# The second layer's matmuls in two halves of 112 columns

## The chip, the core and the metric

The kernel runs on one core of one Trainium2 chip. The metric is the device time of one execution in microseconds (us), median of three runs. The matmuls are float32 throughout.

## The reference

Eight batches of attention with RMS-normed queries and keys, followed by a two-layer block on the 3584 resulting rows of 768 values:

```python
# q, k, v: (8, 12, 448, 64)
q_n, k_n = rmsnorm(q, g_q), rmsnorm(k, g_k)
scores = q_n @ k_n.T / sqrt(64)
attn = softmax(scores)
x = (attn @ v) -> (8 * 448, 12 * 64)

# w_in: (768, 2048), w_out: (2048, 768)
h = x @ w_in
g = h - tanh(h)
out = g @ w_out
```

The first layer is `x @ w_in`, the second `g @ w_out`.

## The kernel before

From the second batch on, both layers are computed with a Strassen-like scheme: the tokens of a batch (448) and the two other dimensions are split in halves, and seven products of half the size in each direction take the place of eight. Each product is a run of matmuls with 128x128 weights and `HS` = 224 columns of tokens, which accumulate in one bank of PSUM. The weights' combinations lie in DRAM and come through a ring of six buffers. In the first batch the second layer is computed without the scheme (`project_first`, line 675, 448 columns).

The matmuls of both layers are issued by one generator, `products`. `layer` is 0 for the first layer (4 blocks `j`, `width` 2, `depth` 3) and 1 for the second (3 blocks `j`, `width` 1, `depth` 8). `moving[p]` gives the tokens' side of product `p`: for the second layer slices of `g` (tile gT) and their combinations (tile tg).

```python
HS = S // 2                                  # 224
ORDER = (1, 5, 6, 2, 3, 7, 4)

def products(b, layer, count, width, depth, moving, done_with):
    took = 4 * HS / ENGINE_NS
    ...
    def product(j, p, bank, first):
        if b == 0:
            ...
        else:
            ring_load(ring_steps.index((b, layer, j, p)) + 5)
            w = ring_tiles[b, layer, j, p].rearrange("p (n d) -> p n d", d=P)
        for f in range(width):
            for c in range(depth):
                nc.tensor.matmul(                                   # line 510
                    bank[:, f * HS : (f + 1) * HS], lhsT=w[:, c * width + f, :], rhs=moving[p](c),
                    start=(first and f == 0 and c == 0), stop=(f == width - 1 and c == depth - 1),
                    skip_group_check=not first,
                )
                if f < width - 1 or c < depth - 1:
                    yield took
    ...
    for j in range(count):
        use = done_with(j)
        for p in ORDER:
            first = p not in (2, 3, 7)
            bank = banks[p] = mm_bank() if first else banks[{2: 1, 3: 5, 7: 6}[p]]
            yield from product(j, p, bank, first)
            use(p, bank)
            yield took
```

The generator is advanced piece by piece between the parts of the attention of the batch ahead, by an estimate of time, not by what is ready:

```python
def run(ns):
    spent[1] += ns
    while spent[0] + 1.0 < spent[1]:
        took = next(stream, None)
        if took is None:
            return
        spent[0] += took

def slot(s):                       # one step of attention, two heads
    gap = gap_ns(s)
    totals(s, sc_bank())           # line 443: sums of the softmax
    if has(s + 1):
        scores(s + 1, 0)           # line 401: 112x448, 64 rows
    ...
    run(gap)
    if has(s + 2):
        turn(s + 2, sc_bank(), sc_bank())      # lines 377 and 381: transposes, 112 columns
    ...
    run(gap)
    divide(s, values(s, sc_bank()))            # line 429: attn @ v
    ...
    run(gap)
    ...
    run(gap)
```

The transposes are matmuls of TensorE too: the block to be turned is the weights' operand, and an identity of 112 columns is the moving one.

Of the kernel before, what the change touches and what calls it, by code (L numbers as in the profile page):

```python
# [92 lines left out]
def bounded_path(tc, ctx, q, k, v, moe_w_in, moe_w_out, out, g_col, ident, ones, neg_half):  # L93
# [16 lines left out]
    nc = tc.nc  # L110
# [12 lines left out]
    HS = S // 2  # L123
# [25 lines left out]
    def mm_bank():  # L149
        return ps_m.tile([P, 512], F32, name="mm")  # L150
# [34 lines left out]
    def built(j, p):  # L185

        if j == 2:
            return ring[:, p * 2 * HALF : (p + 1) * 2 * HALF].rearrange("p (f n) -> p f n", f=2)
        return w_half[j == 1][p]
# [51 lines left out]
    def weight(to):  # L241

        while done[1] < min(to, PIECES):
            n = done[1]
            round_weight_a(nc, raws[n], weight_dst(n))
            if n:
                round_weight_b(nc, raws[n - 1], weight_dst(n - 1))
            done[1] = n + 1
            finish_weights(n)
            while done[0] < min(n + 4, PIECES) and place_free(done[0]):  # L250
                weight_load(done[0])
                done[0] += 1
            if kept[1] < kept[0] and n >= 4 * kept[0] + 2:
                keep_weights()
        if done[1] == PIECES > done[2]:
            round_weight_b(nc, raws[PIECES - 1], weight_dst(PIECES - 1))
            finish_weights(PIECES)
# [15 lines left out]
    def combine(count):  # L273
        for j, p, dst, x, y, op in combos[:count]:
            nc.vector.tensor_tensor(out=dst, in0=x, in1=y, op=op)  # L275
            if p == 7:
                kept[0] = j + 1
        del combos[:count]
# [51 lines left out]
    def ring_load(to):  # L330

        for n in range(len(ring_tiles), min(to, len(ring_steps))):
            b, layer, j, p = ring_steps[n]
            t = ring_tiles[ring_steps[n]] = ring_slot()
            if layer == 0:
                assert kept[1] > j
                nc.sync.dma_start(out=t[:, : 2 * HALF], in_=w_in_dram[j, p])
            else:
                nc.sync.dma_start(out=t, in_=w_out_dram[:, BLOCKS[p], j].rearrange("p f d -> p (f d)"))
# [149 lines left out]
    def products(b, layer, count, width, depth, moving, done_with):  # L489

        took = 4 * HS / ENGINE_NS
        banks = {}

        def product(j, p, bank, first):
            if b == 0:
                weight(due[7 * j + ORDER.index(p)])  # L500
                combine(1)
                while any(c[:2] == (j, p) for c in combos):
                    combine(1)
                w = built(j, p).rearrange("p f (n d) -> p (f n) d", d=P)
            else:
                ring_load(ring_steps.index((b, layer, j, p)) + 5)
                w = ring_tiles[b, layer, j, p].rearrange("p (n d) -> p n d", d=P)
            for f in range(width):
                for c in range(depth):
                    nc.tensor.matmul(  # L510
                        bank[:, f * HS : (f + 1) * HS], lhsT=w[:, c * width + f, :], rhs=moving[p](c),
                        start=(first and f == 0 and c == 0), stop=(f == width - 1 and c == depth - 1),
                        skip_group_check=not first,
                    )
                    if f < width - 1 or c < depth - 1:
                        yield took
            now = late["todo"]
            late["todo"] = []
            for fn in now:
                fn()  # L520
# [9 lines that stand above are left out]
# [570 lines left out]
```

## Time and profile before

| | before |
|---|---|
| time, median of 3 runs | 1482.98 us (1481.69 to 1483.19) |
| span of the profiled execution | 1479.9 us |
| TensorE: matmul busy | 1442.1 us, 97% |
| TensorE: weight load busy | 1142.9 us, 77% |
| VectorE busy | 791.8 us, 54% |
| ScalarE busy | 469.6 us, 32% |
| GpSimd busy | 469.0 us, 32% |
| DMA | 247.32 MB, 167 GB/s |

In the profile PE is TensorE's matmuls and PEld its weight loads, which can lie beside matmuls; DVE is VectorE, ACT ScalarE, POOL GpSimd. A group's row gives line, engine, operation, written tile <- read tiles, the array's rows * columns, the moving operand's partitions x elements, the count, the busy time in us (overlaps counted once), the mean duration of one in ns, and the idle time of the engine just before, with what ended it. A matmul's duration is longer than the time from one to the next, since matmuls are pipelined.

### The profile page before, as it was taken

What the parts mean: (1) busy time and instruction counts of PE and PEld (TensorE: products, weight loads), DVE (VectorE), ACT (ScalarE), POOL (GpSimd) and SP (SyncE); (2) the same over time, 40 slices, a digit from 0 to 9 for tenths busy, and PEclk for the clock granted to TensorE, in tenths of its full rate; (3) what the DMA queues carried; (4) which work ended last, traced back from release to release, by engine and by line L of the source; (5) the groups of instructions that cost most, each with busy time, mean ns of one, the idle gap of its engine ahead of it and who ended that gap; (6) DMA issues with size and microseconds to landing.
All of it is one profiled execution on the core that took longest, in us unless ns stands there. A gap on an engine that the chain in (4) does not pass through costs nothing.

```text
span 1479.9 us, 22097 instructions
## 1 busy us (share of the span) xinstructions
PE 1442.1 (97%) x8520; PEld 1142.9 (77%) x8520; DVE 791.8 (54%) x1165; ACT 469.6 (32%) x850; POOL 469.0 (32%) x336
## 2 busy tenths in 40 slices
PE   6889999999999999999999999999999999999997
PEld 2358744587888788878888887888788878889997
DVE  4889998656543664346534564454555356423322
ACT  6765554233222322232322233223332233200100
POOL 4556664134311343124412243212441134202310
PEclk9999999999999999999999999999999999999999
DMA  9759788854456454645465536545545654465663
GB/s 183 157 154 244 247 238 219 231 169 145 146 171 182 130 175 135 189 136 163 147 177 143 164 127 192 145 127 171 173 147 139 178 167 134 126 177 160 184 195 98
DMA packets 244997, 247.32 MB, mean 167 GB/s; under 512 B 143380, under 2 KB 187156, under 8 KB 244884
## 3 DMA queue, kind: packets, MB, share of 16 engines
q1 hardware_dynamic: 244560, 245.82, 58.0%
q8 instruction: 70, 1.15, 0.3%
q14 instruction: 43, 0.35, 0.1%
q10 hardware_dynamic: 324, 0.00, 0.0%
HBM read 212.34 MB, written 33.42 MB: 166 GB/s over the span
## 4 chain that ended last, share of the span: by engine, by line
PE 86%; DVE 10%; DMA 2%; issue 1%; SPq 0%; POOL 0%; ACT 0%; ACTq 0%; DVEq 0%; POOLq 0%
PE mm L510 60%; PE sc L401 9%; PE sc L429 9%; PE mm L675 3%; DVE sum L420 2%; PE sc L443 2%; DMA q_nat<-in_q_dram 1%; PE sc L381 1%; DVE w_out L79 1%; DVE sum L418 1%; PE sc L377 1%; DVE w_out L82 1%; DVE w_out L78 1%; DVE w_out L275 1%; DVE rr L357 1%
## 5 line engine op out<-in xcount | busy, mean ns | idle before, releaser
L406 ACT ACTIVATE p<-sc,rr 112x448 f32<-112x448 f32 x384 | 212.3, 638 | 480.2 <-PE sc L401 468.2
L510 PE MATMUL mm<-xT,w_f 128*128 128x224 f32 x1392 | 278.8, 355 | 0.0
L510 PEld LDWEIGHTS mm<-xT,w_f 128*128 128x128 f32 x1392 | 260.3, 190 | 17.3 <-issue 12.6
L510 PEld LDWEIGHTS mm<-gT,w_f 128*128 128x128 f32 x1344 | 251.3, 190 | 23.7 <-issue 23.7
L510 PE MATMUL mm<-gT,w_f 128*128 128x224 f32 x1344 | 267.8, 355 | 0.0
L360 POOL TENSOR_TENSOR rr<-rr,neg_half 112x16 f32<-112x16 f32 (+1 forms) x54 | 144.5, 2681 | 259.4 <-DVE rr L359 252.8
L510 PE MATMUL mm<-tt,w_f 128*128 128x224 f32 x1044 | 211.2, 354 | 0.0
L510 PEld LDWEIGHTS mm<-tt,w_f 128*128 128x128 f32 x1044 | 196.1, 190 | 8.0 <-issue 8.0
L510 PE MATMUL mm<-tg,w_f 128*128 128x224 f32 x1008 | 200.4, 353 | 0.0
L510 PEld LDWEIGHTS mm<-tg,w_f 128*128 128x128 f32 x1008 | 189.5, 190 | 0.0
L547 POOL TENSOR_TENSOR gT<-s,th 128x448 f32<-128x448 f32 x96 | 117.3, 1229 | 193.1 <-ACT th L546 192.4
L401 PE MATMUL sc<-qT,kT 64*112 64x448 f32 x768 | 176.3, 573 | 1.6 <-ACT p L406 1.0
L456 DVE TENSOR_TENSOR xT<-sc,rs 64x224 f32<-64x224 f32 x168 | 65.2, 388 | 140.7 <-PE sc L429 137.0
L470 POOL TENSOR_TENSOR tt<-xT,tt 128x224 f32<-128x224 f32 x23 | 15.8, 688 | 391.1 <-DVE xT L456 391.0
L401 PEld LDWEIGHTS sc<-qT,kT 64*112 64x112 f32 x768 | 63.8, 177 | 95.1 <-issue 82.4
L429 PE MATMUL sc<-p,v_nat 112*32 112x448 f32 x1344 | 135.0, 542 | 0.0
L420 DVE TENSOR_TENSOR sum<-sum,p 112x896 f32<-112x896 f32 x78 | 103.0, 1320 | 6.5 <-DVE sum L420 0.5
L429 PEld LDWEIGHTS sc<-p,v_nat 112*32 112x32 f32 x1344 | 39.4, 109 | 74.8 <-issue 73.2
L546 ACT ACTIVATE th<-s 128x448 f32<-128x448 f32 x96 | 55.3, 579 | 106.0 <-DVE s L576 47.6
L675 PE MATMUL mm<-gT,w_out 128*128 128x448 f32 x192 | 74.6, 543 | 0.4 <-POOL w_out L90 0.4
L629 DVE TENSOR_TENSOR s<-mm,s 128x224 f32<-128x224 f32 x21 | 8.2, 392 | 116.2 <-PE mm L510 116.2
L448 DVE RECIPROCAL rs<-sc 128x224 f32<-128x224 f32 x42 | 65.2, 1553 | 1.5 <-PE sc L443 1.2
(97 smaller groups left out, 1323.1 us busy)
## 6 DMA issues: line engine op xcount, KB each, us to landing
w_f<-w_in SPq DMA_DIRECT2D x196, 384.0 KB, 3.7
w_f<-w_out SPq DMA_DIRECT2D x147, 512.0 KB, 4.6
w_raw<-in_moe_w_out_dram SPq DMA_DIRECT2D x16, 768.0 KB, 5.3
k_nat<-in_k_dram SPq DMA_DIRECT2D x96, 112.0 KB, 3.4
q_nat<-in_q_dram SPq DMA_DIRECT2D x48, 224.0 KB, 4.3
v_nat<-in_v_dram SPq DMA_DIRECT2D x48, 224.0 KB, 4.8
out_dram<-th SPq DMA_DIRECT2D x192, 56.0 KB, 2.3
w_in<-w_out SPq DMA_DIRECT2D x21, 384.0 KB, 7.0
```

The source lines that it names most:

```text
L360: nc.gpsimd.tensor_tensor(out=r, in0=r, in1=neg_half[:, : r.shape[1]], op=ALU.pow)
L401: nc.tensor.matmul(sc[:CP, :S], lhsT=kT[r, c * CP : (c + 1) * CP], rhs=qT[r, :], start=True, stop=True)
L406: nc.scalar.activation(p[:, h, i, :], tiles[h][:CP, :S], AF.Exp, scale=rr[:, 0, 2 * c + h : 2 * c + h + 1])
L420: nc.vector.tensor_tensor(out=t, in0=t, in1=part, op=ALU.add)
L429: nc.tensor.matmul(av[r : r + BL, :S], lhsT=v_nat[:, h, c, m * BL : (m + 1) * BL], rhs=p[:, h, c % 2, :], start=(c == 0), stop=(c == NCH - 1),
L443: nc.tensor.matmul(dn[r : r + BL, :HS], lhsT=ones[:CP, :BL], rhs=p[:, h, n * HS : (n + 1) * HS], start=(i == 0), stop=(i == len(parts) - 1),)
L448: nc.vector.reciprocal(rs, dn[:, :HS])
L456: nc.vector.tensor_tensor(out=x[m * D : (m + 1) * D, n * HS : (n + 1) * HS], in0=av[m * D : (m + 1) * D, n * HS : (n + 1) * HS], in1=rs[n ...
L510: nc.tensor.matmul(bank[:, f * HS : (f + 1) * HS], lhsT=w[:, c * width + f, :], rhs=moving[p](c), start=(first and f == 0 and c == 0), sto ...
L546: nc.scalar.activation(th, h, AF.Tanh, bias=0.0, scale=1.0)
L547: eng.tensor_tensor(out=g[:, rows, cols], in0=h, in1=th, op=ALU.subtract)
L675: nc.tensor.matmul(bank[:, :S], lhsT=w_out_row(f, n // HC)[:, n % HC * P : (n % HC + 1) * P], rhs=g[:, f, :], start=(f == 0), stop=(f == C ...
```

## The change

In the second layer of the seven batches that use the seven products, each matmul of 224 columns of tokens becomes two of 112 with the same weights, one for each half of the columns. The two write neighbouring halves of the same stretch of the bank. The first layer, the first batch, the attention and the order of everything else stay as they are. Shorter matmuls give a finer grain: a half's result is there earlier, and the stationary weights serve two matmuls in succession.

```diff
             for f in range(width):
                 for c in range(depth):
-                    nc.tensor.matmul(
-                        bank[:, f * HS : (f + 1) * HS], lhsT=w[:, c * width + f, :], rhs=moving[p](c),
-                        start=(first and f == 0 and c == 0), stop=(f == width - 1 and c == depth - 1),
-                        skip_group_check=not first,
-                    )
+                    m = moving[p](c)
+                    for n in range(0, HS, HS // 2) if layer else (0,):
+                        z = n + HS // 2 if layer else HS
+                        nc.tensor.matmul(
+                            bank[:, f * HS + n : f * HS + z], lhsT=w[:, c * width + f, :], rhs=m[:, n:z],
+                            start=(first and f == 0 and c == 0 and n == 0),
+                            stop=(f == width - 1 and c == depth - 1 and z == HS), skip_group_check=not first,
+                        )
                     if f < width - 1 or c < depth - 1:
                         yield took
```

## The prediction

> **What bounds the kernel now.** I read the page's engine table and slices first, then the chain that ended last, then the list of waits, and then single stretches of the timeline, because the change touches nothing but TensorE and the question is what TensorE's pace consists of.
>
> ```profile
> PE 1442.1 (97%) x8520; PEld 1142.9 (77%) x8520; DVE 791.8 (54%) x1165; ACT 469.6 (32%) x850; POOL 469.0 (32%) x336
> ...
> PEclk9999999999999999999999999999999999999999
> ...
> PE 86%; DVE 10%; DMA 2%; issue 1%; SPq 0%; POOL 0%; ACT 0%; ACTq 0%; DVEq 0%; POOLq 0%
> PE mm L510 60%; PE sc L401 9%; PE sc L429 9%; PE mm L675 3%; DVE sum L420 2%; PE sc L443 2%; DMA q_nat<-in_q_dram 1%; PE sc L381 1%; DVE w_out L79 1%; DVE sum L418 1%; PE sc L377 1%; DVE w_out L82 1%; DVE w_out L78 1%; DVE w_out L275 1%; DVE rr L357 1%
> ```
>
> TensorE is busy 97% of the span at full granted clock, and line 510, the line that is changed, is 60% of the chain. As many weight loads (PEld) as matmuls stand in the table, so every matmul has a load of its own. The list of waits, TensorE alone and from 200 us on, comes to 2.5 us in all:
>
> ```profile
> PE sc L443 <- DVE sum L420: 2.1, 2, 1.6
> PE mm L675 <- POOL w_out L90: 0.4, 1, 0.4
> ```
>
> So after the first batch TensorE runs without a pause. What it gets slower by goes into the time undiminished, and no other engine has to be looked at. The second layer's matmuls are the gT and tg groups:
>
> ```profile
> L510 PE MATMUL mm<-gT,w_f 128*128 128x224 f32 x1344 | 267.8, 355 | 0.0
> L510 PEld LDWEIGHTS mm<-gT,w_f 128*128 128x128 f32 x1344 | 251.3, 190 | 23.7 <-issue 23.7
> L510 PE MATMUL mm<-tg,w_f 128*128 128x224 f32 x1008 | 200.4, 353 | 0.0
> L510 PEld LDWEIGHTS mm<-tg,w_f 128*128 128x128 f32 x1008 | 189.5, 190 | 0.0
> ```
>
> The program has 7 batches x 3 blocks x 7 products x 8 = 1176 such matmul calls, the trace 1344 + 1008 = 2352 records. Each call is thus two passes, and each pass is a load and a matmul. Busy time and duration overlap, so the pace comes from the end of the chain, where line 510 runs alone:
>
> ```profile
> 1334.28 137.93 PE mm L510 x728
> ```
>
> With the last matmul's 0.35 us taken off, 137.58 / 727 = 189.2 ns from one pass to the next. The first batch's matmuls of 448 columns (line 675) follow each other in 376 ns in the trace's records. So a column costs (376 - 189.2) / 224 = 0.834 ns and a pass 2.4 ns besides: the pace is the moving columns', and the load is hidden completely.
>
> **What the Trainium skill says.** "TensorE: Matmul & The Clock Gate", section "LDWEIGHTS (loading the stationary operand)", gives P/1.2 ns for a load of P columns, 107 ns for 128, and the same page, section "Step-by-step: what each phase is for", says that the next tile's weights load while this tile's matmul runs. The trace agrees with both: the load stands beside a 189 ns matmul at no cost, and where it is exposed it costs about what the formula says. In the view of line 510, a matmul's record is 352 ns long in the median and 457 at most:
>
> ```profile
> L510 PE MATMUL mm<-gT,w_f x1344: 352/352/457, 380.2 to 1468.8; 128*128 128x224 f32 x192
> ```
>
> The longest are nearly all the first after the attention's scores (line 401, matmuls on 64 rows), where load and matmul start together in the timeline; the 105 ns more are the load, which nothing hides there. The load's own record of 190 ns is therefore not what it occupies. "Advanced Engine Details and Errata", section "TensorE Details", says that a matmul can start before its load completes. If that held here, those 105 ns would not show; the trace speaks against it for a full 128x128 load.
>
> **The change part by part.** It removes 2352 passes of 224 columns and adds 4704 of 112. The columns streamed are the same; each half brings its weight load again, because a call is a pair of passes with two loads in turn, and the program holds no call without them (the built program has 2352 loads more, as many as matmuls). The order on every engine stays, since the generator yields once per pair and its estimate of the time taken is untouched. DMA, DVE, ACT and GpSimd work is unchanged.
>
> A pass of 112 columns streams in 112 x 0.834 = 93.4 ns, 95.8 with its fixed part. The load for the next pass can begin when the present one starts and needs about 107 ns. For the first time the load is the longer of the two, and the pace becomes the load's. The kernel before contains exactly this pair: the transposes (line 381) are passes of 112 columns, and some are followed at once by a line-510 pass with its 128-column load. Loads at such a place, as the timeline gives them:
>
> ```profile
> 710.29 0.49 PEld L510 LDWEIGHTS mm<-xT,w_f 128*128 128x128 f32 x3
> ```
>
> Three loads of 190 ns cover 0.49 us, so from the first start to the third are 0.30 us. The second of these steps is the ordinary 0.19 us beside a 224-column pass; the first, beside a 112-column transpose, is 0.11. By single records: the transpose starts at 710.289, the load at 710.290, the next load at 710.400, and the matmul between them takes 368 ns instead of 352, 16 ns of waiting for its weights. All 37 such places in the trace give 111 or 112 ns from the transpose to the point where that matmul really streams. I take 111 ns for a pass of the changed stream.
>
> The sum: a pair of halves takes 2 x 111 = 222 ns in place of 189.2, so +32.8 ns, times 2352 = **+77.1 us**. At the ends of the 51 stretches of second-layer work the last half is followed by attention work whose load is short or which has to wait for the matmul's end anyway, so there one half costs 93 to 96 instead of 111: 51 x about 15 ns = -0.8 us. Waits that the slower TensorE could swallow are the 2.5 us above, of which little lies next to the second layer; I count nothing. So +76 us, and 1483 + 76 = 1559; as the loads by themselves are 110 ns apart, which would give +72, I say 1558.
>
> **The rivals.**
> - The load stays hidden, because the second half finds its weights in the array or because a matmul starts on a part of them. A half would then take the 95.8 ns, and the change would cost 2352 x (191.6 - 189.2) = +6 us: 1489, within 2%. For it speaks the skill's sentence and that no call in the kernel before repeats its predecessor's weights at the same place, so that a skipped load could not have been seen. Against it: a call is two passes with two loads, so the weights left in the array at the second half are not those of its first pass; and the 16 ns of waiting at every one of the 37 places.
> - The load is not pipelined at all and holds the array for its 190 ns record. A pair would be 380 ns, +449 us, 1932. Against it stand the overlapping loads just shown, 0.11 us apart.
> - TensorE's instruction supply becomes the bound: two instructions each 111 ns, 55 ns apiece, against 95 before. In attention alone, ahead of the second layer, this stretch did more:
>
> ```profile
> 35.80:47.60 11.80, 11.80 (x128) 5.58 (x130) 10.95 (x20) 10.61 (x20) 5.56 (x4) 1.00 0.64 137
> ```
>
> The first two counts are matmuls and loads: 258 instructions in 11.8 us, 46 ns apiece. The rate is there, though only over 12 us; over a stretch of 150 us it isn't shown. A bound at 60 ns would make it +120 us. The program's own instructions are also fetched by DMA, and 4704 more are some 20% of the 22097; the queue for that takes 0.3% of the transfer time, so I expect nothing.
> - The change helps something: shorter matmuls could release banks sooner or start an eviction earlier. With 2.5 us of waits there is nothing to win; at the very end the last eviction comes after the last half either way.
>
> **Range and chances.** The one uncertain size is the pass of 112 columns. 108.5 ns, the load's bare 107 with a pass's 2 ns, gives +65 us; 112.5 gives +84. With some room for supply, 1549 to 1568 should hold it 8 times in 10. Faster would need a gain that no row offers: 0.01. Within 2%, below 1512.6, is the hidden load: 0.04. Slower by over 2%: 0.95.
>
> **What would show it.** Right: the gT and tg groups with 2688 and 2016 records of 128x112, a pace of 110 to 112 ns for each where they run alone, loads of 190 ns that now overlap each other so that PEld is busy nearly throughout those stretches, matmul records of about 275 ns (the transposes' 259 and 16 of waiting), TensorE still at 97 to 98% and the other engines' busy times unchanged. Wrong: a pace of 96 ns, fewer loads than matmuls, gaps with "issue" ahead of matmuls or loads in those groups, or a granted clock below 1.00.

## The result, and the profile after

The changed kernel takes 1562.4 us (median of 4, 1561.78 to 1564.0) against 1482.8 us of the kernel before (median of 4): 79.6 us more, a ratio of 1.054 (95% interval 1.0522 to 1.0558). The prediction was 1558, with a range of 1549 to 1568.

From the page of the changed kernel, the engine table, the granted clock and the chain that ended last:

```profile
PE 1523.1 (98%) x10872; PEld 1231.0 (79%) x10872; DVE 788.7 (51%) x1165; ACT 469.2 (30%) x850; POOL 469.0 (30%) x336
...
PEclk9999999999999999999999999999999999999999
...
PE 88%; DVE 8%; DMA 1%; issue 1%; ACT 1%; POOL 0%; SPq 0%; ACTq 0%; DVEq 0%; POOLq 0%
```

The only engine whose work grew is TensorE: 81.0 us of matmul busy time and 88.1 us of load busy time. There are 2352 more records of each kind, one load for each added matmul. The line is 513 now. Its second-layer groups (PEld are the loads; count, busy us, mean ns, idle before):

```profile
L513 PEld LDWEIGHTS mm<-gT,w_f 128*128 128x128 f32 x2688 | 304.8, 192 | 23.7 <-issue 16.4
L513 PE MATMUL mm<-gT,w_f 128*128 128x112 f32 x2688 | 313.1, 276 | 0.0
L513 PE MATMUL mm<-tg,w_f 128*128 128x112 f32 x2016 | 234.6, 275 | 0.0
L513 PEld LDWEIGHTS mm<-tg,w_f 128*128 128x128 f32 x2016 | 229.8, 192 | 0.0
```

gT rose from 267.8 to 313.1 us and tg from 200.4 to 234.6: 79.5 us together, as much as the medians differ by. (The two profiled executions differ by 81.3 us; 0.9 us of that is there before the first pass of the second layer's groups.) The idle time ahead of the loads is 23.7 us as before, and no other group grew by more than 0.4 us on the page. The waits of TensorE from 200 us on (us in total, times, longest) come to 2.9 us in place of 2.5:

```profile
PE sc L443 <- DVE sum L420: 2.5, 4, 1.6
PE mm L678 <- POOL w_out L90: 0.4, 1, 0.4
```

So nothing new is waited for; it is the passes that come more slowly. How fast they are can be read in two places. In a stretch of the timeline inside the second layer, loads alone (start and duration in us):

```profile
800.05 0.41 PEld L513 LDWEIGHTS mm<-tg,w_f 128*128 128x128 f32 x3
```

Three loads of 192 ns cover 0.41 us, so they start (0.41 - 0.19) / 2 = 0.11 us apart and each overlaps the next. And at the end of the chain, where line 513 has TensorE to itself:

```profile
1401.33 151.30 PE mm L513 x1120
```

These are 336 passes of 224 columns (the last batch's first layer) and 784 of 112 (its second layer, 672, and the last 112 of the batch ahead). Before, the same work stood there as 728 passes in 137.93 us. The difference is 13.37 us for 392 divided passes: 34.1 ns for each, or (189.2 + 34.1) / 2 = 111.7 ns for a pass of 112 columns. In the records 4614 of 4651 steps inside the two groups are 111 or 112 ns; 36 of the others are 200 ns and follow a first pass whose own load is exposed.

### The profile page after: what moved, and what is told of

Read it like the earlier page. It is cut to its first block, busy times and chain, and to the rows that moved or that the text cites. A ratio compares the mean times of both kernels' runs of the same rounds, so it can differ in the third digit from the quotient of the medians.

```text
span 1561.2 us, 26823 instructions
## 1 busy us (share of the span) xinstructions
PE 1523.1 (98%) x10872; PEld 1231.0 (79%) x10872; DVE 788.7 (51%) x1165; ACT 469.2 (30%) x850; POOL 469.0 (30%) x336
## 3 DMA queue, kind: packets, MB, share of 16 engines
q8 instruction: 88, 1.44, 0.4%
## 4 chain that ended last, share of the span: by engine, by line
PE 88%; DVE 8%; DMA 1%; issue 1%; ACT 1%; POOL 0%; SPq 0%; ACTq 0%; DVEq 0%; POOLq 0%
PE mm L513 63%; PE sc L401 9%; PE sc L429 8%; PE mm L678 3%; PE sc L443 2%; DVE sum L420 2%; PE sc L381 1%; DVE w_out L79 1%; DMA q_nat<-in_q_dram 1%; PE sc L377 1%; DVE w_out L82 1%; DVE sum L418 1%; DVE w_out L78 1%; PE mm L429 1%; DVE rr L357 0%
## 5 line engine op out<-in xcount | busy, mean ns | idle before, releaser
L513 PEld LDWEIGHTS mm<-gT,w_f 128*128 128x128 f32 x2688 | 304.8, 192 | 23.7 <-issue 16.4
L513 PE MATMUL mm<-gT,w_f 128*128 128x112 f32 x2688 | 313.1, 276 | 0.0
L513 PE MATMUL mm<-tg,w_f 128*128 128x112 f32 x2016 | 234.6, 275 | 0.0
L513 PEld LDWEIGHTS mm<-tg,w_f 128*128 128x128 f32 x2016 | 229.8, 192 | 0.0
```

What stands on the lines that cost most here:

```text
L513: nc.tensor.matmul(bank[:, f * HS + n : f * HS + z], lhsT=w[:, c * width + f, :], rhs=m[:, n:z], start=(first and f == 0 and c == 0 and n ...
```

## The experiments

Three readings of these 111.7 ns were put against each other. **L**: a 128-column weight load sets the pace as soon as the moving columns are too few to cover it. **I**: TensorE's instructions can't be supplied faster than about 56 ns each, and there are two to a pass. **F**: a short pass carries a fixed 16 ns whatever its shape. A fourth, **S**, says that it matters that the same weights are loaded twice in a row.

### The pace of passes by shape

The kernel before, with a table of shapes behind its end (results unused):

```diff
     run(1e9)
+    for cols in (128, 96, 64, 32):
+        for n in (224, 160, 128, 112, 64, 32):
+            bank = mm_bank()
+            for i in range(16):
+                nc.tensor.matmul(
+                    bank[:cols, :n], lhsT=ident[:, :cols], rhs=late["g"][:, i, :n], start=(i == 0), stop=(i == 15)
+                )
```

> The kernel before, with 24 groups of 16 matmul calls (32 passes each) put behind its end: weights of 128, 96, 64 and 32 columns, moving operands of 224, 160, 128, 112, 64 and 32. Theory L (the weight load sets the pace of a short pass): a pass takes the longer of the moving columns' time, 0.834 ns each and 2.4 ns, and the load's, 0.834 ns for each weight column and some 5 ns. For 128 weight columns 189, 136, then 112 for 128, 112, 64 and 32 moving columns alike; for 96: 189, 136, 109, 96, then 85 for 64 and 32; for 64: 96 at 112 columns, 58 at 64 and 32; for 32: 96, 56, 31. About 88 us in all, so 1570 us. Rival I (TensorE's supply of instructions, 56 ns for each): no pass under 112 ns at any width of the weights, 99 us in all. Rival F (a fixed 16 ns for a short pass): 112 columns take 112 ns at every width of the weights, 32 columns some 45.

It took 1568.2 us (one run; 1570 were expected). Some groups of the added line; 128*96 means 96 weight columns, the moving operand follows, and busy time less one duration, divided by 31, is the pace (coarse here, because busy time has one decimal):

```profile
L786 PE MATMUL mm<-gT,ident 128*128 128x160 f32 x32 | 4.5, 299 | 0.0
L786 PE MATMUL mm<-gT,ident 128*128 128x112 f32 x32 | 3.7, 275 | 0.0
L786 PE MATMUL mm<-gT,ident 128*128 128x64 f32 x32 | 3.7, 274 | 0.0
L786 PE MATMUL mm<-gT,ident 128*96 128x112 f32 x32 | 3.2, 259 | 0.0
L786 PE MATMUL mm<-gT,ident 128*96 128x64 f32 x32 | 2.9, 247 | 0.0
L786 PE MATMUL mm<-gT,ident 128*64 128x64 f32 x32 | 2.0, 222 | 0.0
L786 PE MATMUL mm<-gT,ident 128*32 128x32 f32 x32 | 1.2, 196 | 0.0
```

With full weights, 64 and 112 moving columns take the same 3.7 us. With 96 weight columns the 112-column group drops to 3.2 us and its matmuls to 259 ns. By single records the median pace in ns is:

| weight columns | 224 moving | 160 | 128 | 112 | 64 | 32 |
|---|---|---|---|---|---|---|
| 128 | 189 | 136 | 112 | 112 | 112 | 112 |
| 96 | 189 | 136 | 109 | 96 | 85 | 85 |
| 64 | 189 | 136 | 109 | 96 | 58 | 58 |
| 32 | 189 | 136 | 109 | 96 | 56 | 32 |

Every entry is that of L within 1 ns. The moving columns cost 0.834 ns each and 2.4 ns; the load costs 0.834 ns a column and 5 ns, which is 111.8, 85.1, 58.4 and 31.7 ns for the four widths; the larger one is the pace. I is out, over stretches as short as these: 32 ns for a pass is 16 ns for an instruction. F is out: 112 columns with 96 weight columns carry no 16 ns.

### Uneven parts

```diff
-                    for n in range(0, HS, HS // 2) if layer else (0,):
-                        z = n + HS // 2 if layer else HS
+                    for n, z in ((0, 160), (160, HS)) if layer else ((0, HS),):
```

> The changed kernel with the halves made uneven, 160 and 64 columns: as many passes, loads and columns. Theory L: the long part takes its columns' 136 ns and hides its load, the short one takes the load's 111.7 ns: 247.5 for both instead of 223.4, times 2352 is +57 us, 1619 us. Rival I: the same, since it is a floor too. Rival F: each part pays for its columns and 16 ns, so the sum is that of the even halves: 1562 us.

Measured: 1617.7 us, ratio to the kernel before 1.0912 (1.0894 to 1.0930). With as many passes, loads and columns as the even halves it is 55.3 us slower than they are. The end of its chain holds the same 1120 passes as that of the changed kernel:

```profile
1445.69 160.74 PE mm L512 x1120
```

160.74 - 151.30 = 9.44 us over 392 pairs is 24.1 ns, exactly 247.5 - 223.4. The long part pays for its columns, the short one for its load, and what the long part has to spare is of no use to the short one. F, which had 1562 us here, is out once more.

### The same weights not twice in a row

Against the changed kernel (the first layer keeps its loop, in an `else` not shown):

```diff
-            for f in range(width):
-                for c in range(depth):
-                    m = moving[p](c)
-                    for n in range(0, HS, HS // 2) if layer else (0,):
-                        ...
+            if layer:
+                for n in (0, HS // 2):
+                    for c in range(depth):
+                        nc.tensor.matmul(
+                            bank[:, n : n + HS // 2], lhsT=w[:, c, :], rhs=moving[p](c)[:, n : n + HS // 2],
+                            ...
+                        )
```

> The changed kernel with the two halves outside the loop over the contraction: first all eight matmuls of one half of the columns, then all eight of the other, so that no two matmuls in a row have the same weights. Theory L: a load costs the same whatever stood in the array before: 1562 us, within 2 us. Rival S (weights that are there already are loaded more cheaply, so the change would have cost more without that; or a repeated load of one place is what costs): more than 5 us away from 1562, in the first case slower, up to the time of a load for every second pass, in the second towards 1489.

Measured: 1562.6 us, ratio 1.0539 (1.0522 to 1.0557), the changed kernel's time to 0.2 us. The two layers have lines of their own here, so the end of the chain separates the first layer (224 columns) and the second (112):

```profile
1413.18 63.58 PE mm L521 x336
1476.76 75.04 PE mm L511 x672
```

63.58 / 336 = 189.2 ns and 75.04 / 672 = 111.7 ns. S is out: with weights that change at every call a pass takes what it takes with weights that come twice.

### The weights in halves instead of the tokens

```diff
-                    nc.tensor.matmul(
-                        bank[:, f * HS : (f + 1) * HS], lhsT=w[:, c * width + f, :], rhs=moving[p](c),
-                        ...
-                    )
+                    for k in range(0, P, P // 2) if layer else (0,):
+                        e = k + P // 2 if layer else P
+                        nc.tensor.matmul(
+                            bank[k:e, f * HS : (f + 1) * HS], lhsT=w[:, c * width + f, k:e], rhs=moving[p](c),
+                            ...
+                        )
```

> The kernel before with the second layer's calls split along the other side: two matmuls of 64 weight columns each, both with all 224 columns of tokens, writing the two halves of the partitions. As many calls, passes and loads as in the changed kernel. Theory L: the loads are half as long and hidden; the two column halves of the array work side by side, as the attention's values do in the trace with four matmuls of 32 weight columns that start 7 ns apart, so a pair takes little more than 189 ns: 1483 to 1500 us. (If the halves did not work side by side it would be about 1930.) Rival I: 4704 passes at 112 ns as in the changed kernel, 1562 us.

Measured: 1487.2 us, ratio 1.0033 (1.0019 to 1.0047). Its groups:

```profile
L512 PE MATMUL mm<-gT,w_f 128*64 128x224 f32 x2688 | 266.3, 354 | 0.0
L512 PE MATMUL mm<-tg,w_f 128*64 128x224 f32 x2016 | 201.4, 353 | 0.0
L512 PEld LDWEIGHTS mm<-gT,w_f 128*64 128x64 f32 x2688 | 190.1, 137 | 81.5 <-issue 16.7 <-PE sc L401 7.3
```

As many passes, loads and instructions as in the changed kernel, but busy times of the kernel before (267.8 and 200.4). The records start in pairs mostly 6 to 8 ns apart, two passes side by side. Four instructions in 189 ns are 47 ns apiece, under the 56 of rival I, and over whole batches: the supply is not what sets the changed kernel's pace. Of the 3.9 us more, 3.0 lie where these stretches meet the transposes: from the last pass to the first transpose 283 ns instead of 189, from the last transpose to the first pass 189 instead of 96, at 16 places each.

This run also shows the load by itself. The longest record, a first pass whose load nothing hides, was 457 ns before, 105 above the median of 352; with half the weight columns it is 52 above:

```profile
L512 PE MATMUL mm<-gT,w_f x2688: 352/352/404, 381.0 to 1472.9; 128*64 128x224 f32 x192
```

So the 105 ns go with the number of weight columns, as a load's time does.

### Dividing where the columns are enough

The second layer of the first batch has matmuls of 448 columns. There the same division can be made with and without dropping below the load:

```diff
-            nc.tensor.matmul(
-                bank[:, :S], lhsT=w_out_row(f, n // HC)[:, n % HC * P : (n % HC + 1) * P], rhs=g[:, f, :],
-                start=(f == 0), stop=(f == CF - 1),
-            )
+            for a in range(0, S, 224):          # 112 in the second run
+                nc.tensor.matmul(
+                    bank[:, a : a + 224], lhsT=w_out_row(f, n // HC)[:, n % HC * P : (n % HC + 1) * P],
+                    rhs=g[:, f, a : a + 224], start=(f == 0 and a == 0), stop=(f == CF - 1 and a + 224 == S),
+                )
```

> The kernel before, with the first batch's second layer (96 calls of 448 columns, 192 passes) in halves of 224 columns; the other batches as before. Theory L: 224 columns hide the load, so a pass of 376 ns becomes two of 189.2 and the cost is 2.4 ns x 192, +0.5 us: the same within 2 us. Rival: halving a matmul costs as such, because the second load has to be paid: 16 ns to 112 ns for each of 192 passes, +3 to +21 us.

> The same calls in four parts of 112 columns. Theory L: 4 x 111.7 in place of 376 ns, +70.8 ns for each of 192 passes: +13.6 us, about 1497 us. A rival in which only the number of passes counts would make this three times the cost of the halves: +1.5 us if those cost 0.5.

In halves of 224: 1482.6 us against 1482.0, ratio 1.0002 (0.9994 to 1.0011). In quarters of 112: 1492.7 us, ratio 1.0073 (1.0059 to 1.0087), +10.6 us. The rows of the divided line, duration as min/median/max, then the first and last start in us; the first is of the run with halves:

```profile
L676 PE MATMUL mm<-gT,w_out x384: 352/352/457, 190.2 to 288.8; 128*128 128x224 f32 x192
```

and the second of the run with quarters:

```profile
L676 PE MATMUL mm<-gT,w_out x768: 275/275/363, 190.3 to 298.5; 128*128 128x112 f32 x192
```

Doubling the loads was free; doubling them once more was not. The quarters' +10.6 us are 3 us under the 13.6 expected. Here, unlike in the later batches, there were waits next to the slower passes which could swallow a part. From 190 to 330 us TensorE waited 3.7 us in the run with halves:

```profile
PE sc L443 <- DVE sum L420: 2.0, 2, 1.5
PE sc L381 <- DVE rs L448: 1.1, 1, 1.1
PE mm L676 <- POOL w_out L90: 0.6, 1, 0.6
```

and 0.5 us in the run with quarters:

```profile
PE sc L443 <- DVE sum L420: 0.5, 1, 0.5
```

The 3.2 us between them are what was missing. (In the kernel before these waits are 2.5 us, but its first pass of line 675 starts only at 192.1 us, against 190.2 and 190.3 us in these two runs.)

## Why the prediction was right

- **What bounds it.** TensorE's pace goes into the time undiminished: the two groups grew by 79.5 us, the time by 79.6. Right. The quarters above show the condition: where waits stand next to the slower passes, a part is swallowed.
- **The pace of a pass.** This was the step that decided, and it was read off the kernel before: 37 places where a 112-column transpose is followed by a full load. Predicted 111 ns, measured 111.7. The term is 2352 x (2 x 111.7 - 189.2) = 80.4 us where 77.1 stood. The 37 places had given it more exactly than it was used: 29 of them show 112 ns and 8 show 111, a mean of 111.8, which makes 1563 us. It was rounded down to 111, and the lean towards 110 ns, which turned 1559 into 1558, went the wrong way too: in the steady stream the loads start 111 or 112 ns apart.
- **The ends of the stretches**, -0.8 us: the right size in the wrong place. By single records the second layer's stretches, each from its first pass to the start of what follows, take 531.6 us in place of 452.0: 79.6 more, 0.8 under 80.4. But the last half costs its full pace: what follows it starts after 205 ns in place of 282.5 or, for transposes, after 112 in place of 189, which is 77 less each time, the difference between a pass of 111.7 ns and one of 189.2. The saving lies at the starts, some 16 ns at each of 52. After transposes the kernel before had already paid the 16 ns of waiting. At the other 36 the first pass's own load is exposed, and from the first pass to the second it costs 88 ns above the pace (200 - 112) in place of 104 (293 - 189). That the sum was right is luck.
- **The matmul's record**, 259 + 16 = 275 ns: right, the mean of tg is 275.
- **The rivals.** A load that stays hidden is out by the result (1489). One that is not pipelined is out as well (1932; loads overlap by 80 ns). Instruction supply, left open over long stretches, is out by the shape table and by the weights in halves. Shorter matmuls brought nothing: TensorE's waits are 2.9 us in place of 2.5, and no other engine's busy time changed by more than 3.1 us.
- **Instruction fetching.** The page's instruction queue went from 70 to 88 packets, 1.15 to 1.44 MB, at 0.4% of the transfer time; no new wait of TensorE answers to it.

## What to carry to other kernels

Before cutting a matmul's moving side, compare two paces: the moving columns' and the weight load's. Here a float32 pass of a 128x128 matmul needs, by estimate, (111.7 - 2.4) / 0.834 = 131 moving columns to hide its load (128 columns still took 112 ns, 160 hid it). A division whose parts stay above that costs next to nothing (448 into 224); below it every part pays for a full load, however few columns it has. A pass with room to spare doesn't lend it to the one after.

The number of weight columns alone doesn't give the load's pace. The transposes of the kernel before have 128 weight columns too, on 112 rows, and 112 moving columns:

```profile
710.10 0.45 PE L381 MATMUL sc<-ident,n 112*128 112x112 f32 x3
L381 PEld LDWEIGHTS sc<-ident,n 112*128 112x128 f32 x192 | 20.6, 143 | 12.4 <-ACT kT L379 6.8 <-issue 4.3 <-ACT w_out L71 0.9
```

Three of 0.26 us cover 0.45, so they start 0.096 us apart, the pace of their moving columns: these loads, with records of 143 ns where a full one has 190, stay hidden. The prediction passes over this. Whether it is the fewer rows or that they are transposes isn't shown; the formula above is for the matmuls measured.

What a hidden load costs can be read elsewhere in the same trace: look for a short matmul ahead of a full load, such as a transpose, and read how long the next matmul waits.

## What the runs showed of the hardware that was not expected

In the shape table the load's record is much longer than what it occupies: 192, 163, 137 and 110 ns for 128, 96, 64 and 32 columns against a pace of 111.7, 85, 58 and 32. A full row of loads in the profile need not mean that loads are the limit (records of 190 ns every 189 ns before, with no cost). Nor does the share of the span say when they are: it went from 77% only to 79% when the second layer's passes became bound by them.

In the shape table TensorE's granted clock also fell once while it was issuing without a pause. With 32 moving columns in every 112 ns, the records stretch from 1497.0 us on, and for some 3.4 us passes took about twice as long, 224-column ones 373 ns instead of 189. Two stretches, the second with that fall; the columns are those of busy time for each engine, then the granted clock:

```profile
1490.00:1494.00 4.00, 4.00 (x38) 4.00 (x38) 0.00 (x0) 0.00 (x0) 0.00 (x0) 1.00 0.00 0
1494.00:1500.00 6.00, 6.00 (x39) 5.55 (x39) 0.00 (x0) 0.00 (x0) 0.00 (x0) 0.76 0.01 3
```

Before it lay 3.1 us in which the array was given columns for 27 of every 112 ns, by the 0.834 ns a column. Whether that low use caused the drop isn't shown: it is one drop in one run. The changed kernel, with 93 of 112, kept a clock of 1.00 in the second layer.
